# Attention and MoE on one core: the last chunk's stores cut into transfers of 32 rows on two queues, its two halves of tokens summed one after the other

## The chip, the cores and the metric

The kernel runs on one core of a Trainium2 chip. The metric is the device time of one execution in microseconds (us). The time before is 1025.86 us, the median of three runs (1025.6, 1025.86 and 1030.05).

## What is computed

The inputs are q, k and v, each 8 batches x 8 heads x 576 positions x 64, and the weights of a two-layer block. The attention is a sum of two parts, one over keys averaged in groups of four and one over a window of seven positions; its result, turned to 4608 tokens of 512 numbers, goes through the block:

```python
def _attn_ref(q, k, v):
    q_d = q.reshape(B, H, Sd, factor, D).mean(axis=3)        # k_d, v_d likewise
    out_up = np.repeat(sm_attn(q_d, k_d, v_d), factor, axis=2)
    mask = np.abs(pos[:, None] - pos[None, :]) < factor
    ...
    return (out_up + out_local).astype(np.float32)

def _moe_ref(x, w_in, w_out, alpha):                          # 4608x512, 512x2048, 2048x512
    h = x @ w_in
    g = np.maximum(h, 0.0) + alpha * np.minimum(h, 0.0)
    return (g @ w_out).astype(np.float32)
```

## The kernel before

The 4608 tokens are worked on in 18 chunks of 256 (`T`, `NCHUNK`). The hidden dimension of 2048 is taken in 8 pairs of 128 (`NP`), so that there are 144 steps (`NS`), eight to a chunk. One step has five parts: `hidden` (24 matmuls in three terms, since both factors are held as a high and a low part), `slopes` on ScalarE, `larger` on VectorE, `split` (the high part on ScalarE, the low part on GpSimd, the tiles `gh` and `gl`) and `product` (line 786), which multiplies by the second weight matrix and adds into two PSUM tiles of 128 tokens x 512, `o` in the profile. These two tiles are the two halves of tokens of a chunk, m = 0 and m = 1. They take the sum over all eight steps of the chunk.

The order of all instructions is written out by hand: each part is put down with a due time by `at`, in units of one step, and the list is sorted and emitted (lines 847 to 854 and 901 to 903). `finish` (line 799) stands 0.42 of a step after the last `product` of its chunk. Attention work for later chunks lies between the steps; it is all over before the last chunks, whose steps follow each other with nothing between.

In `product` (lines 791 to 797) the loops run over the two blocks j of the pair, the three terms i (`gh` with the high weights, `gh` with the low ones, `gl` with the high ones) and the two halves m, with m innermost. A step therefore issues 12 matmuls that go to the two PSUM tiles in turn, and the sums of both halves are complete only with the last two.

`finish` copies each half from PSUM to a staging tile `sg` on ScalarE (line 802) and stores it from SyncE's queue (line 805). Where the rows go is decided by `rows` (line 773). Tokens of the first 576 positions lie in the output's order, and their store is one run of rows. All later chunks hold their tokens in another order: 192 positions are six rows of the sequence by 32 places that are 18 rows apart. For these, `rows` yields patterns such as

```python
                u, o = divmod(pos, 192)
                m = min(n, 192 - o)
                row = (u // 3) * S + 6 * (u % 3) + o // 32
                ap = bass.AP(out.tensor, row * DM, [[DM, m // 32], [SEG * DM, 32], [1, DM]])
```

in which the outermost count is m // 32. The last chunk starts at position 4352, which is 128 positions into a group of 192. Its half m = 0 is stored as 64 rows (2 x 32) and then 64 rows of the next group (2 x 32), its half m = 1 as 128 rows (4 x 32). A row of the output is 2 KB, so these three transfers have 128, 128 and 256 KB. Chunks 0 and 1 are stored as runs of 128 rows.

Of the kernel before, what the change touches and what calls it, by code (L numbers as in the profile page):

```python
# [9 lines left out]
F32 = mybir.dt.float32  # L10
# [7 lines left out]
DM, DF = 512, 2048  # L18
# [7 lines left out]
NF = DF // 128  # L26
T = 256
# [6 lines left out]
SB = 2  # L34
# [16 lines left out]
def tile_attention_moe(ctx: ExitStack, tc: tile.TileContext, q, k, v, w_in, w_out, alpha, out):  # L51
    nc = tc.nc
# [3 lines left out]
    two = ctx.enter_context(tc.tile_pool(name="two", bufs=2))  # L56
# [17 lines left out]
    NS = NCHUNK * NF // 2  # L74
    NP = NF // 2
# [41 lines left out]
    wi, wo = ([[None] * 4, [None] * 4] for _ in range(2))  # L117
# [623 lines left out]
    gs, outs, hs = {}, {}, {}  # L741
# [31 lines left out]
    def rows(pos, n):  # L773
        while n:
            if pos < S:
                m = min(n, S - pos)
                ap = bass.AP(out.tensor, pos * DM, [[DM, m], [1, DM]])
            else:
# [4 lines that stand above are left out]
            yield m, ap  # L783
            pos, n = pos + m, n - m

    def product(st):
        c, fp = divmod(st, NP)
        if fp == 0:
            outs[c] = [ps_o.tile([128, DM], F32, tag="po", name=f"o{c}_{m}") for m in range(T // 128)]
        gh, gl = gs.pop(st)  # L790
        for j in range(2):
            f = 2 * fp + j
            n, o = divmod(f, 4)
            for i, (g, w) in enumerate(((gh, 0), (gh, 1), (gl, 0))):
                for m, po in enumerate(outs[c]):
                    nc.tensor.matmul(po, g[:, j, 128 * m:128 * m + 128], wo[w][n][:, o, :],  # L796
                                     start=(f == 0 and i == 0), stop=(f == NF - 1 and i == 2))

    def finish(c):
        for m, po in enumerate(outs.pop(c)):  # L800
            sg = two.tile([128, DM], F32, tag="stage", name=f"sg{c}_{m}", bufs=SB)
            nc.scalar.copy(sg, po)
            row = 0
            for cnt, ap in rows(T * c + 128 * m, 128):
                nc.sync.dma_start(ap, sg[row:row + cnt, :])
                row += cnt

    def place_rest():
        hi, lo = (t[:, :, 0:S - 2 * T] for t in operand(2))
        nc.scalar.copy(hi, rest)  # L810
        sub(lo, rest, f32(hi))
# [7 lines left out]
    with tc.tile_pool(name="start", bufs=1) as start:  # L819
        load_pair, load_windows, pair = first_batch(start)  # L820
        todo = [(w, fp) for fp in range(NP) for w in range(2)]
        for step in ORDER.split():
            kind, i = step[0], int(step[1])
# [16 lines left out]
        def at(t, f, *args):  # L840
            events.append((t, len(events), f, args))
# [5 lines left out]
    for s in range(NS):  # L847
        at(s - 1.95, hidden, s)
        at(s - 1.45, slopes, s)
        at(s - 1.15, larger, s)  # L850
        at(s - 1.0, split, s)
        at(s + 0.6, product, s)
        if s % NP == NP - 1:
            at(s + 1.02, finish, s // NP)

    blocks = [(w, fp, c) for w in range(2) for fp in range(N_EARLY, NP) for c in range(2)]
    at(-1.98, load_raw, 0, N_EARLY)
# [71 lines left out]
```

## Time and profile before

| what | value |
|---|---|
| median of three runs | 1025.86 us (1025.6 to 1030.05) |
| the profiled execution | 1026.39 us |
| its span, from the first to the last instruction | 1024.5 us |
| mean granted TensorE clock | 0.969 |
| TensorE busy | 960.5 us, 94% of the span |
| VectorE, ScalarE, GpSimd busy | 81%, 55%, 48% |
| share of the 16 DMA engines, last six of 40 slices of the span | 1 0 0 0 0 0 tenths |

The table's lines come from the page of the profile and its list of cores. The time of an execution is 1.89 us above its span, which lies around what the profiler sees. In the views, a row of the timeline gives the start in the span, the length, the engine, the line of the kernel, the operation, the tiles written and read and, behind an x, how many instructions it merges. A row of the table of windows gives a stretch of the span, its length, the busy time of each engine with its number of instructions, the granted clock, the share of the 16 DMA engines that were busy, and the GB/s that they moved; a share of 0.25 stands for four engines. `SPq` is SyncE's queue, on which line 805 issues; issuing instructions do not count as busy. Line 925 is the end of the program, where SyncE waits for the last transfers.

### The profile page before, as it was taken

The page shows a single profiled execution, that of the slowest core. Times are in us where ns is not written, and L with a number is a line of the kernel's source. Part 1 is how long each engine was busy: PE and PEld are TensorE (multiplying, and loading weights), DVE is VectorE, ACT ScalarE, POOL GpSimd, SP SyncE. Part 2 cuts the span into 40 slices and gives each one's busy share as a digit, 9 for nine tenths or more (in the row PEclk, how much of TensorE's full clock was granted, in tenths as well). Part 3 has the DMA queues.
Part 4 walks back from the last instruction along what each step waited for, and adds up shares of the span by engine and source line. Part 5 has one row for each costly group of instructions (what it writes and reads, how often), then busy time and mean ns, then how long its engine had stood idle before and what let it go on. Part 6 is the DMA issues. An engine that isn't in the chain of part 4 may idle for free.

```text
span 1024.5 us, 17852 instructions
## 1 busy us (share of the span) xinstructions
PE 960.5 (94%) x6402; PEld 853.0 (83%) x6402; DVE 831.8 (81%) x1346; ACT 560.4 (55%) x1484; POOL 487.7 (48%) x612
## 2 busy tenths in 40 slices
PE   4877989999999999999999999999999999999995
PEld 4756868898888899988888888888888898989894
DVE  6899978898788899899879888898898899995110
ACT  4767766465555554555555554655555564444442
POOL 2160645676565645555555544655555542333221
PEclk9956989999999999999999999999999999999998
DMA  8947343232322322322322232322322221100000
GB/s 184 228 141 246 111 126 110 96 109 85 115 100 95 106 75 86 109 93 102 107 84 74 92 107 77 116 90 80 104 98 81 93 78 62 73 36 21 1 21 20
DMA packets 59549, 98.25 MB, mean 96 GB/s; under 512 B 19910, under 2 KB 25286, under 8 KB 59462
## 3 DMA queue, kind: packets, MB, share of 16 engines
q1 hardware_dynamic: 59462, 97.12, 30.1%
q8 instruction: 50, 0.82, 0.3%
q14 instruction: 37, 0.30, 0.1%
HBM read 87.67 MB, written 9.44 MB: 95 GB/s over the span
## 4 chain that ended last, share of the span: by engine, by line
PE 74%; DVE 12%; DMA 4%; ACT 3%; issue 2%; SPq 2%; POOL 2%; ACTq 0%; DVEq 0%; POOLq 0%
PE h L752 34%; PE o L796 33%; PE s L263 2%; PE pv L297 2%; DVE temp L193 2%; DMA raw<-in_moe_w_in 1%; PE xp L659 1%; DMA ld<-in_v 1%; PE pT L287 1%; DVE temp L194 1%; DMA k<-in_k 1%; DVE t L764 1%; DVE qk L591 1%; SPq L393 1%; DVE temp L188 1%
## 5 line engine op out<-in xcount | busy, mean ns | idle before, releaser
L69 POOL TENSOR_TENSOR gl<-t,gh 128x512 fp32r<-128x512 f32 x144 | 186.4, 1295 | 312.9 <-ACT gh L769 281.5
L760 ACT ACTIVATE t<-h,slope 128x256 f32<-128x256 f32 x288 | 136.3, 473 | 205.4 <-PE h L752 163.6
L72 POOL TENSOR_TENSOR ld<-ld 72x256 f32<-72x256 f32 x168 | 130.8, 779 | 158.4 <-DMA ld<-in_q 88.6
L752 PE MATMUL h<-xh,wih 128*128 128x256 f32 x1152 | 191.9, 288 | 0.7 <-ACT xh L518 0.7
L764 DVE TENSOR_TENSOR t<-h,t 128x512 f32<-128x512 f32 x144 | 99.0, 687 | 114.8 <-ACT h L761 112.9
L796 PE MATMUL o<-woh,gh 128*128 128x512 f32 x576 | 187.5, 407 | 0.4 <-ACT woh L203 0.4
L752 PE MATMUL h<-xl,wih 128*128 128x256 f32 x1152 | 184.3, 282 | 1.4 <-POOL xl L69 1.4
L752 PE MATMUL h<-xh,wil 128*128 128x256 f32 x1152 | 185.0, 283 | 0.0
L796 PE MATMUL o<-woh,gl 128*128 128x512 f32 x576 | 181.1, 396 | 0.9 <-POOL gl L69 0.9
L796 PE MATMUL o<-wol,gh 128*128 128x512 f32 x576 | 181.4, 396 | 0.2 <-DVE wol L211 0.2
L752 PEld LDWEIGHTS h<-xh,wih 128*128 128x128 f32 x1152 | 164.2, 191 | 10.7 <-issue 1.8
L752 PEld LDWEIGHTS h<-xl,wih 128*128 128x128 f32 x1152 | 157.5, 190 | 1.6 <-POOL xl L69 1.6
L752 PEld LDWEIGHTS h<-xh,wil 128*128 128x128 f32 x1152 | 158.4, 191 | 0.0
L769 ACT CAST gh<-t 128x512 fp32r<-128x512 f32 x144 | 89.1, 619 | 120.7 <-DVE t L764 71.4
L595 DVE TENSOR_REDUCE ls<-qk 128x12 f32<-128x768 f32 (+1 forms) x126 | 136.4, 1082 | 2.8
L796 PEld LDWEIGHTS o<-woh,gl 128*128 128x128 f32 x576 | 108.2, 188 | 27.5 <-POOL gl L69 1.3
L796 PEld LDWEIGHTS o<-wol,gh 128*128 128x128 f32 x576 | 108.1, 188 | 26.8 <-DVE wol L211 1.1
L761 ACT ACTIVATE h<-h,sign 128x256 f32<-128x256 f32 x288 | 126.4, 439 | 0.0
L650 DVE TENSOR_TENSOR lb<-lb,pv 128x384 f32<-128x384 f32 x202 | 113.9, 564 | 5.5
L796 PEld LDWEIGHTS o<-woh,gh 128*128 128x128 f32 x576 | 98.1, 189 | 16.2 <-issue 2.2
L647 DVE TENSOR_TENSOR pv<-v,lb 128x1152 f32<-128x1152 f32 x84 | 93.6, 1115 | 2.6
L591 DVE TENSOR_TENSOR qk<-k,qp 128x768 f32<-128x768 f32 (+1 forms) x78 | 84.1, 1079 | 0.6 <-DMA k<-in_k 0.6
(146 smaller groups left out, 1108.6 us busy)
## 6 DMA issues: line engine op xcount, KB each, us to landing
k<-in_k SPq DMA_DIRECT2D x41, 384.0 KB
v<-in_v SPq DMA_DIRECT2D x41, 384.0 KB
raw<-in_moe_w_in SPq DMA_DIRECT2D x16, 512.0 KB
raw<-in_moe_w_out SPq DMA_DIRECT2D x16, 512.0 KB
ld<-in_q SPq DMA_DIRECT2D x56, 144.0 KB
ld<-in_k SPq DMA_DIRECT2D x56, 144.0 KB
ld<-in_v SPq DMA_DIRECT2D x56, 144.0 KB
q<-in_q SPq DMA_DIRECT2D x42, 192.0 KB
```

Source lines behind the costliest of these rows:

```text
L69: nc.gpsimd.tensor_tensor(o, a, b, op=ALU.subtract)
L72: nc.gpsimd.tensor_tensor(o, a, b, op=ALU.add)
L591: nc.vector.tensor_tensor(st["pr"][:, :nd], window(tiles[u, "k"], half, d0, nd), st["qp", half].unsqueeze(1).to_broadcast([128, nd, 2, 192 ...
L595: nc.vector.tensor_reduce(out=st["s"][:, half, d0:d0 + nd, :].rearrange("p a b -> p (a b)"), in_=st["pr"][:, :nd].rearrange("p a h (t d) - ...
L647: nc.vector.tensor_tensor(st["pr"][:, :nd], window4(tiles[u, "v"], half, d0, nd), prob(half, d0, nd), op=ALU.mult)
L650: nc.vector.tensor_tensor(st["acc"], st["acc"], st["pr"][:, i], op=ALU.add)
L752: nc.tensor.matmul(ph[:, j], w[:, m, 128 * o:128 * o + 128], x[:, m, :], start=(i == 0), stop=(i == 11))
L760: nc.scalar.activation(t[:, j], hs[st][:, j], AF.Copy, scale=slope[:, f:f + 1])
L761: nc.scalar.activation(hs[st][:, j], hs[st][:, j], AF.Copy, scale=sign[:, f:f + 1])
L764: nc.vector.tensor_tensor(gs[st], hs.pop(st), gs[st], op=ALU.max)
L769: nc.scalar.copy(gh, t)
L796: nc.tensor.matmul(po, g[:, j, 128 * m:128 * m + 128], wo[w][n][:, o, :], start=(f == 0 and i == 0), stop=(f == NF - 1 and i == 2))
```

## The change

Three things change, all in the last chunk alone. In the last step (`NS - 1`) `product` sorts its 12 matmuls by the half m, so that the six of m = 0 come first and the six of m = 1 after them; within a half, the order stays. In all other steps the order is the same as before. The last chunk is stored by a new function `finish_last`, at the same due time as `finish`: it copies half 0 on ScalarE and half 1 on VectorE, and it stores each half as four transfers of 32 rows (64 KB), the first and third from SyncE's queue and the second and fourth from ScalarE's queue. `rows` yields for 32 rows a pattern whose outermost count is 1: `[[DM, 1], [SEG * DM, 32], [1, DM]]`. No other transfer of the kernel is issued from ScalarE's queue.

```diff
-        for j in range(2):
+        order = [(j, i, m) for j in range(2) for i in range(3) for m in range(T // 128)]
+        if st == NS - 1:
+            order.sort(key=lambda x: x[2])
+        for j, i, m in order:
             f = 2 * fp + j
             n, o = divmod(f, 4)
-            for i, (g, w) in enumerate(((gh, 0), (gh, 1), (gl, 0))):
-                for m, po in enumerate(outs[c]):
-                    nc.tensor.matmul(po, g[:, j, 128 * m:128 * m + 128], wo[w][n][:, o, :],
-                                     start=(f == 0 and i == 0), stop=(f == NF - 1 and i == 2))
+            g, w = ((gh, 0), (gh, 1), (gl, 0))[i]
+            nc.tensor.matmul(outs[c][m], g[:, j, 128 * m:128 * m + 128], wo[w][n][:, o, :],
+                             start=(f == 0 and i == 0), stop=(f == NF - 1 and i == 2))
...
+    def finish_last(c):
+        for m, po in enumerate(outs.pop(c)):
+            sg = two.tile([128, DM], F32, tag="stage", name=f"sg{c}_{m}", bufs=SB)
+            if m == 0:
+                nc.scalar.copy(sg, po)
+            else:
+                nc.vector.tensor_copy(sg, po)
+            for i in range(4):
+                (_, ap), = rows(T * c + 128 * m + 32 * i, 32)
+                (nc.sync if i % 2 == 0 else nc.scalar).dma_start(ap, sg[32 * i:32 * i + 32, :])
...
-            at(s + 1.02, finish, s // NP)
+            at(s + 1.02, finish if s + 1 < NS else finish_last, s // NP)
```

## The prediction

> **What bounds the kernel now.** The edit touches only the last step of the last chunk and its stores, so the profile is read there. I started with the page's head, then took the timeline of the last microseconds.
>
> ```profile
> span 1024.5 us, 17852 instructions
> ```
> ```profile
> 1009.45 0.63 PE L796 MATMUL o<-woh,gh 128*128 128x512 f32 x2
> 1011.78 0.62 PE L796 MATMUL o<-woh,gl 128*128 128x512 f32 x2
> 1012.22 1.07 ACT L802 COPY sg<-o 128x512 f32<-128x512 f32 x2 [4.95 <-PE o L796]
> 1012.83 1.79 SPq L805 DMA_DIRECT2D out<-sg  x3
> ```
>
> Of the last product's twelve matmuls the first pair and the last pair are shown: the 11th starts 2.33 us after the first, so 0.233 us lie from one to the next. TensorE is done at 1012.4. The two copies end at 1013.29, the three stores are issued by 1014.62, and yet the span goes on to 1024.5. So 11.2 us from the last copy on have no engine at work. The chain of waits that ended last stops at ScalarE's queue and shows nothing of this; the waits of SyncE and the instructions of the program's end do.
>
> ```profile
> SPq L925 <- DMA out<-sg: 8.8, 3, 3.5
> ```
> ```profile
> L925 SPq EVENT_SEMAPHORE  x1: 28/28/28, 1018.2 to 1018.2; - x1
> L925 SPq EVENT_SEMAPHORE  x1: 28/28/28, 1021.1 to 1021.1; - x1
> L925 SPq EVENT_SEMAPHORE  x1: 28/28/28, 1023.6 to 1023.6; - x1
> ```
>
> The three releases (last two fields: when) are the landings of the three stores, at 1018.2, 1021.1 and 1023.6. The landing at 1023.6 ends the kernel, and 0.9 us of closing work follow. What sets these landings is seen in windows cut at the right places: first the stores of chunk 0, then those of chunk 16, then the tail.
>
> ```profile
> 162.20:163.00 0.80, 0.00 (x0) 0.00 (x0) 0.80 (x2) 0.80 (x3) 0.80 (x1) 1.00 0.00 0
> 163.00:164.40 1.40, 1.33 (x9) 1.18 (x10) 1.37 (x2) 1.37 (x5) 0.02 (x1) 1.00 1.01 350
> 975.00:977.00 2.00, 2.00 (x15) 1.77 (x14) 0.00 (x0) 0.91 (x3) 0.00 (x0) 1.00 0.21 22
> 977.00:982.00 5.00, 5.00 (x35) 4.60 (x34) 0.69 (x1) 1.64 (x4) 1.29 (x1) 1.00 0.25 93
> 1013.00:1014.00 1.00, 0.00 (x0) 0.00 (x0) 0.00 (x0) 0.29 (x1) 0.00 (x0) 1.00 0.00 0
> 1014.00:1016.00 2.00, 0.00 (x0) 0.00 (x0) 0.00 (x0) 0.00 (x0) 0.00 (x0) 0.65 0.12 25
> 1016.00:1021.50 5.50, 0.00 (x0) 0.00 (x0) 0.00 (x0) 0.00 (x0) 0.00 (x0) 0.50 0.23 71
> 1021.50:1023.00 1.50, 0.00 (x0) 0.00 (x0) 0.00 (x0) 0.00 (x0) 0.00 (x0) 0.50 0.13 51
> 1023.00:1023.20 0.20, 0.00 (x0) 0.00 (x0) 0.00 (x0) 0.00 (x0) 0.00 (x0) 0.50 0.13 51
> 1023.20:1024.50 1.30, 0.00 (x0) 0.00 (x0) 0.00 (x0) 0.00 (x0) 0.00 (x0) 0.50 0.00 0
> ```
>
> The last two fields are the share of the 16 DMA engines and the GB/s. Chunk 0's stores, runs of 128 rows, fill all 16 engines (1.01, 350 GB/s). Chunk 16's, whose outermost count is 4, run on four (0.25, 93 GB/s). The tail has two stores of outermost count 2 and one of 4: it runs at up to four engines (0.23) and ends on two (0.13, 51 GB/s). So the outermost count of the pattern is the number of engines, and they are the same ones each time: two engines carry 32 + 32 + 32 = 96 of the last chunk's 256 rows each. 96 rows of 2 KB at 25.5 GB/s (half of 51) are 7.7 us, and the 9.2 us from 1014.0 to 1023.2 are these plus a slow start, which is the row of 1014 to 1016 (25 GB/s). Bound now: two DMA engines, after all compute is over.
>
> **The change part by part.** Further rows for the prices:
>
> ```profile
> 1007.35 1.29 POOL L69 TENSOR_TENSOR gl<-t,gh 128x512 fp32r<-128x512 f32 x1 [4.30 <-ACT gh L769]
> ```
> ```profile
> 1012.22 0.59 ACT L802 COPY sg<-o 128x512 f32<-128x512 f32 x1 [4.95 <-PE o L796]
> ```
> ```profile
> 1009.45 0.40 PE L796 MATMUL o<-woh,gh 128*128 128x512 f32 x1
> ```
> ```profile
> 1012.83 0.55 SPq L805 DMA_DIRECT2D out<-sg  x1
> ```
> ```profile
> L764 DVE TENSOR_TENSOR t<-h,t 128x512 f32<-128x512 f32 x144 | 99.0, 687 | 114.8 <-ACT h L761 112.9 <-POOL pv L627 0.8 <-POOL xl L69 0.3
> L653 DVE TENSOR_TENSOR x<-lb,pv 128x384 f32<-128x384 f32 x42 | 23.4, 557 | 6.0 <-POOL pv L72 2.2
> ```
> ```profile
> 162.18 0.85 SPq L805 DMA_DIRECT2D out<-sg  x2
> ```
> ```profile
> 944.00:974.00 30.00, 30.00 (x194) 27.09 (x193) 4.15 (x6) 12.23 (x28) 6.77 (x6) 1.00 0.00 1
> 983.00:1012.00 29.00, 29.00 (x173) 25.53 (x173) 3.45 (x5) 9.94 (x23) 6.47 (x5) 1.00 0.00 1
> ```
> ```profile
> 897.04 0.78 SPq L545 DMA_DIRECT2D v<-in_v  x1
> 899.81 0.23 SPq L547 DMA_DIRECT2D v<-in_v  x1
> ```
> ```profile
> 1001.21 2.80 PE h L752 x24
> ```
>
> *The order of the sums.* Twelve matmuls stay twelve, so half 1 is complete at 1012.41 as now. Half 0 is complete with the sixth matmul: it starts at 1009.45 + 5 x 0.233 = 1010.62 and ends 0.40 later at 1011.02, where now the 11th ends at 1011.78 + 0.40 = 1012.18. That is 1.16 us earlier. Two things could spoil it. The third matmul now needs `gl` (at 1009.92, where it was the fifth, at 1010.38); GpSimd has it at 1007.35 + 1.29 = 1008.64, so 1.28 us of cover are left. And six matmuls in a row add into one PSUM tile instead of two in turn. `hidden` does that already, twelve in a row into one region, and its 24 matmuls of half the width take 2.80 us, the same 0.117 us per 256 columns as 0.233 per 512. I take nothing for it.
>
> *The copies.* Now ScalarE starts 0.04 us after half 0 is summed (1012.22 against 1012.18), copies for 0.59 and the issue follows 0.02 to 0.03 later. After the change: copy 1011.06 to 1011.65, stores of half 0 issued from 1011.68. Half 1 goes to VectorE, which has nothing left to do. A copy of 128x512 from PSUM by VectorE is not in the trace; the nearest rows are 0.56 (three quarters of the width, two operands) and 0.69 (`larger`, the same width, from PSUM). I take 0.69: 1012.45 to 1013.14, issue at 1013.17. ScalarE's second copy ended at 1013.29, so this gains 0.15.
>
> *The issues.* Eight in place of three, four on each queue. On SyncE one takes 0.23 to 0.78 us by the rows; a three-level pattern like these takes 0.55, and 0.57 from start to start. ScalarE issues none in this trace; I price its issues as SyncE's, 0.57, with the same bounds. Half 0's are then at 1011.68 and 1012.25 on each queue, over by 1012.82, ahead of half 1's, at 1013.17 and 1013.74. On ScalarE the second pair waits for VectorE's copy, but behind it stands only the end of the program. The same holds on SyncE. From an issue to the first bytes the tail shows 1.17 us (1012.83 to 1014.0), chunk 0 shows 0.8. So the first bytes move at 1012.85, and the last transfer's can start at 1013.74 + 1.17 = 1014.91.
>
> *The data.* 32 rows have an outermost count of 1, then 32 with a step. Taken as 32, they can be dealt to 16 engines, two rows each, and all eight transfers put 16 rows on every engine instead of 96 on two. This is the term that matters, and the trace shows 16 engines for stores only in a pattern without the leading 1. At chunk 0's rate 524 KB take 524 / 350 = 1.50 us. Whether the slow start comes back is open: chunk 0's stores, after a short pause, have none; chunks 16 and 17, each after some 30 us with next to no transfer (1 GB/s in the rows from 944 and from 983), both have it, 2.0 us at 22 and 25 GB/s, whether four engines take part or two. I take it as it stands there, 2.0 us in which 50 KB move, so from 1012.85 to 1014.85. Then 474 KB at 350 GB/s take 1.35 us: last bytes at 1016.2. This is later than the 1014.91 + 0.37 (two transfers, 131 KB at 350) = 1015.28 which the issues allow, so a wrong price of an issue or of VectorE's copy is hidden up to 0.9 us.
>
> [...]
>
> *The end.* From the last bytes (1023.2) to SyncE's release (1023.6) are 0.4 us, and 0.9 to the end of the span. So: 1016.2 + 0.4 + 0.9 = 1017.5 in place of 1024.5, **7.0 us less**. The profiled execution took 1026.39, and its forecast is 1019.4. It stands 0.53 above the median of 1025.86; the forecast of the median is **1018.9 us**. Without the slow start the issues bind: 1015.28 + 1.3 = 1016.6, 7.9 less, 1018.0; with issues at 0.23 another 0.3 less, and with chunk 0's 0.8 to the first bytes 0.4 less, 1017.3.
>
> **The rivals.** A measurement of this kernel can tell about 0.5%, 5.1 us, from no change; faster is below 1020.7, slower above 1031.
>
> *One queue's worth of issues.* If the two queues share what makes their transfers, or ScalarE issues at half speed, the eight issues follow each other: half 0's until 1011.68 + 4 x 0.57 = 1013.96, half 1's last at 1013.96 + 3 x 0.57 = 1015.67, first bytes at 1016.84, 64 KB in 0.19, then 1.3: 1018.3. That is 6.2 us less, 1019.7, still faster. For it: nothing here shows two queues at once. [...] Chance 0.15.
>
> *A slow start for each half.* If the slow start belongs to each new burst or to each queue's first use, half 0 takes 1012.85 + 2.0 + (262 - 50) / 350 = 1015.46, and half 1 the same 2.61 again, 1018.07, with the end 1019.4: 5.1 less, 1020.8, right at the bound. Against it: in the tail of before the third store, issued at 1014.1, shows no second slow stretch (71 GB/s from 1016 on). For it: twelve engines and a queue that have been idle for long. Chance 0.12, half of it faster and half the same.
>
> *One engine.* The counts 2, 4 and 128 gave 2, 4 and 16 engines; a count of 1 may give one. Then 256 rows go over one engine: 50 KB in the slow start to 1014.85, 474 KB at 25.5 GB/s 18.6 us, 1033.4, with the end 1034.7: 10.2 more, 1036.1. It decides at two engines: with two, 474 / 51 = 9.3 us end at 1025.4, about as now. For it: the rule as the trace shows it, taken to the letter. Against it: a count of one deals out nothing, and 32 stands next to it. Chance 0.06, slower.
>
> *The cut is worth nothing.* If smaller transfers still wait on the same engines for the same 9.2 us, only the earlier start counts: 1.16 us less, 1024.7, the same. [...] Chance 0.03.
>
> **How the numbers follow.** The forecast has 0.64. Faster: 0.64 + 0.15 + 0.06 = 0.85; the same 0.06 + 0.03 = 0.09; slower 0.06. The range goes from 1017.2, a little below the case without slow start and with cheap issues, to 1021.0, which takes in both rivals above the forecast; one engine and the last rival, 0.09, stay outside, and the rest to 0.2 is for the scatter of runs (one of before is at 1030.05).
>
> **What would show it.** Right: half 0's copy starts near 1011.06, VectorE's takes about 0.69, four issues stand on ScalarE's queue at about 0.55, the DMA share goes to 0.9 or more after a slow first stretch, and SyncE's last release comes near 1016.6. Wrong: a share of 0.06 for 20 us (one engine), issues on ScalarE of over 1.1 us or in turn with SyncE's, a second slow stretch near 1015, or a last release after 1018.5, which would leave less than 5.1 us.

## The result, and the profile after

The changed kernel took 1022.28 us, the median of 16 runs (1017.95 to 1030.71). The kernel before, run beside it, took 1029.08 us, also the median of 16 (1025.6 to 1035.75). The ratio is 0.9934, with a 95% interval from 0.9912 to 0.9956: faster by 0.66%, or 6.8 us (4.5 to 9.1 by the interval). The forecast was a gain of 7.0 us and a time of 1018.9 us, with a range from 1017.2 to 1021.0. So the gain came about as forecast, and the time lies 1.3 us above the range, because the time that the gain was taken from was not 1025.86. One later run of the changed kernel, 1181.21 us at a granted clock of 0.749, is left out of its median and ratio below.

The profiled execution of the changed kernel took 1021.87 us with a span of 1020.0. That span is 4.5 us shorter, not 7. To see why, the span is cut in two at the end of the last matmul. First the timeline of the end of the changed kernel (columns as before; SPq and ACTq are the two queues that issue transfers):

```profile
span 1020.0 us, 17859 instructions
```
```profile
1013.71 0.59 ACT L815 COPY sg<-o 128x512 f32<-128x512 f32 x1 [3.78 <-PE o L798]
1014.32 2.29 SPq L820 DMA_DIRECT2D out<-sg  x4
1014.32 2.36 ACTq L820 DMA_DIRECT2D out<-sg  x4
...
1014.67 0.40 PE L798 MATMUL o<-woh,gl 128*128 128x512 f32 x1
1015.11 0.69 DVE L817 COPY sg<-o 128x512 f32<-128x512 f32 x1 [5.89 <-PE o L798]
```

The last matmul ends at 1015.07, and the span goes on for 1020.0 - 1015.07 = 4.9 us. Before, it ended at 1011.78 + 0.62 = 1012.40 and the span went on for 12.1 us. This stretch, called the tail from here on, became 7.2 us shorter. But the last matmul itself came 2.7 us later. Nothing that the change touches lies ahead of it except the order of its own step. Where the 2.7 us arose is seen by the copies that close chunks 10, 11 and 16 (counted from 0), before (line 802) and after (line 804, the same line of the kernel after the edit):

```profile
680.31 1.07 ACT L802 COPY sg<-o 128x512 f32<-128x512 f32 x2
...
733.18 1.06 ACT L802 COPY sg<-o 128x512 f32<-128x512 f32 x2
...
973.51 1.06 ACT L802 COPY sg<-o 128x512 f32<-128x512 f32 x2
```
```profile
681.39 1.07 ACT L804 COPY sg<-o 128x512 f32<-128x512 f32 x2
...
735.84 1.06 ACT L804 COPY sg<-o 128x512 f32<-128x512 f32 x2
...
976.17 1.06 ACT L804 COPY sg<-o 128x512 f32<-128x512 f32 x2
```

The changed kernel is 1.08 us late at 681, 2.66 at 736, and 2.66 still at 976. The windows between the first two, before and then after, show what goes with the second step: TensorE's granted clock (third field from the end) fell for some 8 us in the second execution (0.83 and 0.74) and not in the first (1.00), which costs about 0.17 x 4 + 0.26 x 4 = 1.7 us by an estimate from these clocks alone; the step between the two copies is 1.58 us.

```profile
684.00:688.00 4.00, 2.60 (x15) 2.16 (x15) 3.60 (x10) 2.66 (x9) 0.00 (x0) 1.00 0.33 99
688.00:692.00 4.00, 4.00 (x33) 3.87 (x32) 3.29 (x5) 0.96 (x2) 2.97 (x4) 1.00 0.38 136
```
```profile
684.00:688.00 4.00, 2.60 (x18) 1.95 (x18) 3.53 (x13) 3.44 (x11) 0.49 (x1) 0.83 0.35 104
688.00:692.00 4.00, 4.00 (x18) 3.29 (x17) 3.83 (x6) 0.69 (x2) 0.35 (x1) 0.74 0.42 138
```

Such a fall is not peculiar to the changed kernel: near 535 us both profiles show one (0.79 and 0.78 in the two windows of 4 us from 531 on before, 0.76 and 0.82 after), each worth about 1.7 us by the same estimate. Whether the one near 688 would have come without the change, these two profiles don't show. The first 1.08 us arose ahead of 631 us without such a difference of the clock: the changed kernel was still 0.53 us early at the stores of chunk 8 (issued from 578.61, before from 579.14) and 1.08 late at those of chunk 9 (631.87 against 630.79), and from 544 to 632 the clock was 1.00 in both profiles. This was not traced. In the profiles of all kernels told of here the last matmul ends anywhere from 1010.6 to 1016.3 us. The tails of the two kernels that were profiled twice came back within 0.1 us. All experiments are therefore read by their tails. But two kernels with the same code in the tail can differ by 1.0 us there, as the last experiment shows, so a difference of less than that is not put down to an edit with certainty. The windows of the changed tail:

```profile
1014.30:1015.10 0.80, 0.77 (x4) 0.29 (x2) 0.00 (x0) 0.00 (x0) 0.00 (x0) 1.00 0.00 0
1015.10:1016.30 1.20, 0.00 (x0) 0.00 (x0) 0.69 (x1) 0.00 (x0) 0.00 (x0) 1.00 0.86 219
1016.30:1016.60 0.30, 0.00 (x0) 0.00 (x0) 0.00 (x0) 0.00 (x0) 0.00 (x0) 1.00 0.01 0
1016.60:1017.80 1.20, 0.00 (x0) 0.00 (x0) 0.00 (x0) 0.00 (x0) 0.00 (x0) 0.98 0.86 220
1017.80:1018.40 0.60, 0.00 (x0) 0.00 (x0) 0.00 (x0) 0.00 (x0) 0.00 (x0) 0.50 0.07 10
1018.40:1020.00 1.60, 0.00 (x0) 0.00 (x0) 0.00 (x0) 0.00 (x0) 0.00 (x0) 0.50 0.00 0
```

The share stands at 0.86 where it was 0.12 to 0.23. The view of DMA queues for the tail, before and then after, says the same in another way: before there were 256 rows and 8 short packets, as many as the three transfers had engines (2 + 2 + 4). Now the short packets are 128, which is 16 for each of eight transfers. The one packet more belongs to an instruction transfer, of which more below.

```profile
DMA packets 264, 0.52 MB, mean 46 GB/s; under 512 B 8, under 2 KB 8, under 8 KB 264
```
```profile
DMA packets 385, 0.53 MB, mean 107 GB/s; under 512 B 128, under 2 KB 128, under 8 KB 384
```

### The profile page after: what moved, and what is told of

It is laid out like the page before. It is cut to its first block, busy times and chain, and to the rows that moved or that the text cites. A ratio compares the mean times of both kernels' runs of the same rounds, so it can differ in the third digit from the quotient of the medians.

```text
span 1020.0 us, 17859 instructions
## 1 busy us (share of the span) xinstructions
PE 961.8 (94%) x6402; PEld 853.0 (84%) x6402; DVE 832.9 (82%) x1347; ACT 560.0 (55%) x1483; POOL 487.6 (48%) x612
## 4 chain that ended last, share of the span: by engine, by line
PE 71%; DVE 12%; DMA 5%; ACT 5%; issue 2%; POOL 2%; SPq 2%; ACTq 0%; DVEq 0%; POOLq 0%
PE h L752 33%; PE o L798 32%; DMA ld<-in_v 3%; PE s L263 2%; PE pv L297 1%; DVE temp L193 1%; DVE t L764 1%; PE xp L659 1%; DVE qk L591 1%; DMA k<-in_k 1%; PE pT L287 1%; DVE temp L194 1%; DVE ls L595 1%; ACT t L760 1%; DMA raw<-in_moe_w_in 1%
## 5 line engine op out<-in xcount | busy, mean ns | idle before, releaser
L72 POOL TENSOR_TENSOR ld<-ld 72x256 f32<-72x256 f32 x168 | 130.7, 778 | 154.7 <-DMA ld<-in_q 78.7
```

The lines of the kernel that those rows point to most:

```text
L72: nc.gpsimd.tensor_tensor(o, a, b, op=ALU.add)
```

## The experiments

The theory was that the number of DMA engines that carry the last rows is nearly the whole gain. Its rivals were the earlier sum of half 0 with the second queue, and, for the slow start, engines that had been idle. Each tail below is the end of the span less the end of the last matmul (start plus length of the last matmul row).

**The cut alone.** The changed kernel with the new order, VectorE's copy and the second queue undone.

```diff
-        if st == NS - 1:
-            order.sort(key=lambda x: x[2])
...
-            if m == 0:
-                nc.scalar.copy(sg, po)
-            else:
-                nc.vector.tensor_copy(sg, po)
+            nc.scalar.copy(sg, po)
...
-                (nc.sync if i % 2 == 0 else nc.scalar).dma_start(ap, sg[32 * i:32 * i + 32, :])
+                nc.sync.dma_start(ap, sg[32 * i:32 * i + 32, :])
```

> The last chunk's stores in transfers of 32 rows, all eight from SyncE; the order of the sums and both copies on ScalarE as before. Read as the tail, from the end of the last matmul to the end of the span: 12.1 us before, 4.9 us after the change. Theory (the number of DMA engines that carry the rows is nearly the whole gain): eight issues one behind the other at 0.39 us from 0.43 on, the last starts 3.2 us after the last matmul, then 2.75 to the release and 1.0 to the end as in the changed kernel: tail 6.9 us, time 5 us below before. Rival (the gain is the earlier sum and the second queue): the cut alone leaves the tail at 11 us or more and the time unchanged.

```profile
span 1022.4 us, 17857 instructions
```
```profile
1015.37 0.62 PE L796 MATMUL o<-woh,gl 128*128 128x512 f32 x2
...
1016.41 3.62 SPq L815 DMA_DIRECT2D out<-sg  x8
```
```profile
1017.20:1020.90 3.70, 0.00 (x0) 0.00 (x0) 0.00 (x0) 0.00 (x0) 0.00 (x0) 0.72 0.57 142
```

The tail is 1022.4 - 1015.99 = 6.4 us, 5.7 of the 7.2 us. The time was 1023.01 us against 1027.34, ratio 0.9961 (0.9941 to 0.9982). Eight issues in 3.62 us set the pace: 64 KB every 0.45 us are 145 GB/s, near the 142 of the window. On top of the cut, the order, VectorE's copy and the second queue together bring the remaining 1.5 us.

**All but the cut.** The changed kernel with the transfers of before, dealt to the two queues in turn.

```diff
-            for i in range(4):
-                (_, ap), = rows(T * c + 128 * m + 32 * i, 32)
-                (nc.sync if i % 2 == 0 else nc.scalar).dma_start(ap, sg[32 * i:32 * i + 32, :])
+            row = 0
+            for i, (cnt, ap) in enumerate(rows(T * c + 128 * m, 128)):
+                (nc.sync if i % 2 == 0 else nc.scalar).dma_start(ap, sg[row:row + cnt, :])
+                row += cnt
```

> The changed kernel with the transfers of before (64, 64 and 128 rows): sums one after the other, half 1 copied by VectorE, stores dealt to two queues in turn. Theory: two engines still carry 96 rows each, so only the earlier start of half 0 counts, 1.2 us: tail 10.9 us, time about 1 us below before. Rival (the gain is the earlier sum and the second queue): tail 5 to 6 us, time 6 us below before.

```profile
span 1023.7 us, 17854 instructions
```
```profile
1011.42 0.40 PE L798 MATMUL o<-woh,gl 128*128 128x512 f32 x1
```
```profile
1012.70:1014.70 2.00, 0.00 (x0) 0.00 (x0) 0.00 (x0) 0.00 (x0) 0.00 (x0) 0.89 0.12 35
1014.70:1016.70 2.00, 0.00 (x0) 0.00 (x0) 0.00 (x0) 0.00 (x0) 0.00 (x0) 0.50 0.22 29
1016.70:1020.20 3.50, 0.00 (x0) 0.00 (x0) 0.00 (x0) 0.00 (x0) 0.00 (x0) 0.50 0.25 84
```

The tail is 11.9 us, and the time did not move: 1027.47 us, ratio 1.0007 (0.9981 to 1.0034). The theory expected 10.9. Half 0 did start earlier, but a second slow stretch (29 GB/s) came with half 1; that it took the 1.2 us back fits, and was not tested by itself. The rival that gave the gain to order and queue falls.

**The old order.** The changed kernel without the sort of the last step.

```diff
-        if st == NS - 1:
-            order.sort(key=lambda x: x[2])
```

> The changed kernel with the old order of the last step's matmuls (the halves in turn). Theory: the last two issues of each queue wait behind half 0's, which come 1.2 us later; the last one starts 1.7 instead of 1.2 us after the last matmul: tail 5.4 us against 4.9. Rival (the order is worth the 1.2 us by which half 0 is earlier): 6.1 us.

```profile
span 1018.7 us, 17859 instructions
```
```profile
1012.62 0.63 PE L796 MATMUL o<-woh,gl 128*128 128x512 f32 x2
```

The tail is 1018.7 - 1013.25 = 5.45 us, 0.5 longer than the changed kernel's, near the theory's 5.4 and not the rival's 6.1. The size is uncertain: the last issue on ScalarE took 0.89 us here, where the others took 0.40 to 0.44, and that alone is about as long as the difference.

**One queue.** The changed kernel with all transfers from SyncE.

```diff
-                (nc.sync if i % 2 == 0 else nc.scalar).dma_start(ap, sg[32 * i:32 * i + 32, :])
+                nc.sync.dma_start(ap, sg[32 * i:32 * i + 32, :])
```

> The changed kernel with all eight transfers issued by SyncE. Theory: half 0's four issues end 0.8 us after the last matmul, half 1's last one starts at 2.0 instead of 1.2 us: tail 5.7 us against 4.9. Rival (both queues feed the same engines, so the second is worth nothing): 4.9 us.

```profile
span 1021.4 us, 17858 instructions
```
```profile
1015.35 3.60 SPq L820 DMA_DIRECT2D out<-sg  x8
...
1015.71 0.40 PE L798 MATMUL o<-woh,gl 128*128 128x512 f32 x1
```

The tail is 5.3 us, 0.4 longer than the changed kernel's, half of what the theory said. So small a difference, from one profile, doesn't rule out the rival.

**Runs of 128 rows.** The kernel before, with each half of the last chunk stored as one run of 128 rows; these rows land in other places of the output than they should.

```diff
-            for cnt, ap in rows(T * c + 128 * m, 128):
+            p0 = T * c + 128 * m
+            run = [(128, bass.AP(out.tensor, p0 * DM, [[DM, 128], [1, DM]]))]
+            for cnt, ap in (run if c == NCHUNK - 1 else rows(p0, 128)):
```

> The kernel before, but each half of the last chunk stored as one run of 128 rows (outermost count 128, as chunks 0 and 1 are), so these rows land in other places of the output than they should. Sums, copies and queue as before; two issues instead of three. Theory (number of engines): issues at 0.4 and 0.9 us after the last matmul, first bytes at 1.2, 524 KB at 350 GB/s to 2.8, 0.6 to the release and 1.0 to the end: tail 4.5 us without any cut, second queue or new order. Rival (small transfers are what helps): tail of 8 us or more; with a slow start as before 5.5 to 6.5.

```profile
span 1020.5 us, 17852 instructions
```
```profile
1015.72 0.62 PE L796 MATMUL o<-woh,gl 128*128 128x512 f32 x2
...
1016.76 0.85 SPq L807 DMA_DIRECT2D out<-sg  x2
```
```profile
1017.60:1019.00 1.40, 0.00 (x0) 0.00 (x0) 0.00 (x0) 0.00 (x0) 0.00 (x0) 0.93 0.98 369
```

The tail is 4.2 us with the old order, one queue, ScalarE's copies and only two issues. Against the cut alone (6.4 us), which has the same order, queue and copies, that is 2.2 us less. So here two transfers of 256 KB were no hindrance (share 0.98, 369 GB/s), and eight of 64 KB from the same queue were no help in themselves (0.57, 142 GB/s); the cut is one way to a pattern that uses 16 engines.

**Runs of 122 and 6 rows.** The same with each half as two runs, the larger of 122 = 2 x 61 rows. These rows too land in other places than they should.

```diff
+            run = [(n, bass.AP(out.tensor, (p0 + r) * DM, [[DM, n], [1, DM]])) for r, n in ((0, 122), (122, 6))]
```

> The kernel before, each half of the last chunk stored as two runs of neighbouring rows, 122 and 6, so these rows land in other places of the output than they should. By the counts 122 rows go to two engines (122 = 2 x 61). Theory (the number of engines sets the tail, whatever the pattern): 124 rows of 2 KB on each of two engines at 25.5 GB/s take 9.9 us, tail 12.8 us, with a slow start 13.8; against 4.2 measured for one run of 128. The slow start: if it belongs to few engines, the first 2 us move about 50 KB again; if it belongs to patterns of three levels (2 or 4 groups of rows 18 apart), they move the full 100 KB. Rival (contiguous rows are what made the runs of 128 quick): tail about 4.5 us.

```profile
span 1029.7 us, 17854 instructions
```
```profile
1014.86 0.62 PE L796 MATMUL o<-woh,gl 128*128 128x512 f32 x2
```
```profile
1016.80:1018.80 2.00, 0.00 (x0) 0.00 (x0) 0.00 (x0) 0.00 (x0) 0.00 (x0) 0.92 0.22 32
1018.80:1027.50 8.70, 0.00 (x0) 0.00 (x0) 0.00 (x0) 0.00 (x0) 0.00 (x0) 0.50 0.14 49
```

The tail is 1029.7 - 1015.48 = 14.2 us. Neighbouring rows from the same queue, but a share of 0.14, two engines, and 49 GB/s, where the runs of 128 rows had 0.98 and 369. The short packets in this tail are 16, as many as two for each run of 122 rows and six for each run of 6 make. That 122 rows go to two engines was the author's estimate until this run; it shows that neither a large count of rows nor their being neighbours was enough for 16. The slow start is there too (32 GB/s for 2 us), so in this run it came without a pattern of three levels.

**Engines kept awake.** The kernel before, with a load of 768 KB that nobody reads just ahead of the last stores.

```diff
+    def awake():
+        kt = late.tile([128, 2, 12, 64], F32, tag="kt", name="awake")
+        flat = kt.rearrange("p h t d -> p (h t d)")
+        nc.gpsimd.memset(flat[:, 0:1], 0.0)
+        nc.sync.dma_start(flat, bass.AP(q.tensor, 0, [[1536, 128], [1, 1536]]))
+
+    at(NS - 1 - 0.9, awake)
```

> The kernel before with one load of 768 KB on 16 engines put ahead of the last chunk's stores, released by GpSimd after the last low part, so that the DMA engines are busy until about 1 us before the first store. Its data is read by nobody. Theory a (the slow start comes from engines that were idle for long): the first 2 us of the stores move about 100 KB instead of 50, and the tail goes from 12.1 to about 11.1 us. Theory b (it belongs to transfers dealt to two or four engines, as the changed kernel's quick start after the same idle time suggests): slow start and tail stay, 12.1 us.

```profile
1007.60:1010.80 3.20, 3.02 (x13) 2.09 (x12) 0.00 (x0) 0.37 (x1) 0.00 (x0) 1.00 0.68 246
1010.80:1012.00 1.20, 0.00 (x0) 0.00 (x0) 0.00 (x0) 0.70 (x2) 0.00 (x0) 1.00 0.00 0
1012.00:1014.00 2.00, 0.00 (x0) 0.00 (x0) 0.00 (x0) 0.00 (x0) 0.00 (x0) 0.84 0.11 20
```

The engines worked until 1010.8, and the stores still began at 20 GB/s. The tail was 11.7 us (span 1022.3, last matmul over at 1010.61), 0.4 less than before. So idleness of over 1.2 us isn't needed for the slow start.

**Both copies on ScalarE.** The changed kernel without VectorE's copy.

```diff
-            if m == 0:
-                nc.scalar.copy(sg, po)
-            else:
-                nc.vector.tensor_copy(sg, po)
+            nc.scalar.copy(sg, po)
```

> The changed kernel with both halves copied by ScalarE (half 1 no longer by VectorE); order, transfers and queues as changed. ScalarE's copy takes 0.59 against VectorE's 0.69 us and comes free 0.1 us before it is needed, so by the copies alone the tail would be 4.8 against 4.9 us. Besides this: in both profiles of the changed kernel an instruction transfer runs among the last rows, and the last two rows of its DMA engine come 0.3 us apart, 0.6 us behind all others; the kernel with the loads cut as well has no such transfer there and a tail of 3.9. Theory (VectorE's additional instruction draws that transfer): it is gone and the tail is 3.8 to 4.0 us. Rival (VectorE's copy has nothing to do with it): the transfer stays and the tail is 4.7 to 4.9.

```profile
span 1020.0 us, 17858 instructions
```
```profile
1015.27 0.40 PE L798 MATMUL o<-woh,gl 128*128 128x512 f32 x1
...
1015.88 0.58 ACT L814 COPY sg<-o 128x512 f32<-128x512 f32 x1 [0.99 <-PE o L798]
```

The tail is 4.3 us against 4.9, although the copy starts 0.2 us late behind ScalarE's own issues. The instruction transfer is gone from among the rows, and so is the gap ahead of the last of them. The time was 1020.51 us, ratio 0.9917 (0.9887 to 0.9947), which cannot be told from the changed kernel's. The tail did not fall to the 3.8 to 4.0 that was expected. Nor does VectorE's copy by itself draw the transfer in: the kernel with the loads cut (below) has the copy, no transfer there, and a tail of 3.9 to 4.0 us, 0.3 to 0.4 less than this one. So the longer tail of the changed kernel goes with the transfer, and not with the copy. That the transfer causes it is not shown, and what draws it in is open.

**Tokens by place.** The changed kernel with the last chunk's tokens reordered when `gh` and `gl` are made, so that 64 rows have an outermost count of 32.

```diff
+        if st >= NS - NP:
+            t = t.rearrange("p j (g a b) -> p (j g) b a", a=2, b=32)
+            gh, gl = (x.rearrange("p j (g b a) -> p (j g) b a", a=2, b=32) for x in (gh, gl))
...
+            for i in range(2):
+                (_, ap), = rows(T * c + 128 * m + 64 * i, 64)
+                ap = bass.AP(out.tensor, ap.offset, [[SEG * DM, 32], [1, 2 * DM]])
+                (nc.sync if i == 0 else nc.scalar).dma_start(ap.rearrange("b (a d) -> b a d", a=2), sg[64 * i:64 * i + 64, :])
```

> The changed kernel with the tokens of the last chunk put in another order when the high and low parts are made (two neighbouring rows side by side), so that a transfer of 64 rows has an outermost count of 32: one issue per queue and half in place of two. Theory (engines, and behind them the issues on the path): the last issue starts 0.8 instead of 1.2 us after the last matmul, tail 4.2 to 4.5 us against 4.9. Rival (transfers of 64 rows are slower in themselves): tail of 4.9 us or more. In the time of the whole kernel the two differ too little to tell.

The tail was 4.8 us (span 1017.0, last matmul over at 1012.20), no better: an issue of this pattern took 0.55 to 0.65 us, which eats most of what the saved one was worth. An instruction transfer and late last rows are in this tail too, so the two cannot be weighed against each other. Ratio 0.9913 (0.9882 to 0.9944).

**The loads cut as well.** The changed kernel with the loads of q, k and v for the later batches in transfers of 32 partitions. The edit for k and v is shown, that for q is alike.

```diff
-                nc.sync.dma_start(flat, bass.AP(src.tensor, off,
-                                                [[2 * HEAD, 4], [SEG * D, 32], [1, 768]]))
+                for a in range(4):
+                    nc.sync.dma_start(flat[32 * a:32 * a + 32],
+                                      bass.AP(src.tensor, off + a * 2 * HEAD, [[SEG * D, 32], [1, 768]]))
```

> The changed kernel with the loads of q, k and v for all later batches cut the same way, into transfers of 32 partitions, all from SyncE. Theory (four engines are too few for these loads as well, and GpSimd's waits for loads behind them reach TensorE): these waits shrink and the last matmul ends 2 to 5 us earlier, ratio to before 0.989 to 0.992. Rival (these loads lie off the path, and four times as many issues clog SyncE's queue): last matmul not earlier, ratio 0.993 or above.

It took 1019.75 us, ratio 0.9905 (0.9875 to 0.9935). GpSimd's waits for loads of q went from 78.7 us in the changed kernel (88.6 before) to 56.4, but the last matmul ended at 1013.58, in the middle of the others. The tail was 3.9 us. To tell it from the changed kernel both ran once more side by side:

> The changed kernel once more, beside the one with the loads in transfers of 32 partitions as well. If the tail is what the change is worth, about 7 us of 1029: ratio 0.993, tail between 3.9 and 4.9 us.

> The changed kernel with the loads of q, k and v in transfers of 32 partitions, once more. If more engines for these loads help the body: ratio 0.003 or more below that of the changed kernel in the same call. If the loads lie off the path: within 0.002 of it.

The changed kernel took 1020.93 us (seven runs), ratio 0.9923 (0.9895 to 0.9951), tail 4.9; the one with the loads cut 1018.83, ratio 0.9903 (0.9874 to 0.9933), tail 4.0. The ratios are 0.002 apart, just at the bound that was set, and half of that is the tail, in whose code the two don't differ. A gain in the body is not shown.

**The tails together.** The instruction transfer is a row `q14 instruction` in the view of DMA queues. This table says where one fell among the last rows.

| kernel | tail, us | instruction transfer among the last rows |
|---|---|---|
| before | 12.1 | no |
| all but the cut | 11.9 | yes |
| the cut alone | 6.4 | no |
| changed (two profiles) | 4.9, 4.9 | yes |
| old order | 5.45 | yes |
| one queue | 5.3 | yes |
| tokens by place | 4.8 | yes |
| both copies on ScalarE | 4.3 | no |
| runs of 128 rows | 4.2 | no |
| the loads cut as well (two profiles) | 3.9, 4.0 | no |
| engines kept awake | 11.7 | no |
| runs of 122 and 6 rows | 14.2 | no |

The changed kernel and the one with the loads cut have the same code for the tail, and 1.0 us lies between them. The steps of 2 us and more in the table are well above this. The worths of the order and of the second queue, each read by itself, are not. Taken together they are: between the cut alone and both copies on ScalarE, which have no such transfer and differ in the order and the second queue, lie 2.1 us.

## Why the prediction was right and its range wrong

*What bounds the end.* Right. Two engines carried 96 rows each (0.13 and 51 GB/s at the end of before), and giving the rows to 16 engines (0.86 and 220 GB/s) took 7.2 us off the tail, forecast 7.0. The cut alone gives 5.7 of it and all else without the cut 0.2. One sum there was loose: 7.7 us and a slow start, which costs about 1.0 us (50 KB in 2.0 us instead of at 51 GB/s), make 8.7 and not 9.2.

*The pattern with a leading 1.* It was dealt to 16 engines; the rival of one engine falls by the share of 0.86 and the 128 short packets. That 32 rows go to 16 engines was the author's estimate; no store of the kernel before has that count, and the changed kernel shows it. In the stores looked at here, outermost counts of 2 (share 0.13), 4 (0.25) and 122 (0.14) went with two or four engines, counts of 32 (0.86) and 128 (1.01 for chunk 0, 0.98 for the last chunk) with 16. So the outermost count is not by itself the number of engines; what sets this number for other counts was not shown.

*Order, copies, issues.* Half 0's copy began 1.36 us before the end of the last matmul, forecast 1.35; VectorE's took 0.69 us, forecast 0.69. ScalarE's issues took 0.38 to 0.44 us and SyncE's 0.31 to 0.41, forecast 0.55; that price came from patterns of three levels, with a leading 2 or 4, and the other pattern of three levels, that of the tokens by place, took 0.55 to 0.65 again.

*The data and the end.* Here several terms were off, and that 7.0 came so near to 7.2 is luck: they cancelled. The slow start of 2.0 us did not come: the first 1.2 us moved 219 GB/s. The first bytes came 0.8 us after the issue, not 1.17. Against this the rate was 220 GB/s, not 350, with a pause of 0.3 us between the halves, and the last few rows came 0.6 us behind the others. Counted from the end of the last matmul, the last bytes came at 3.2 us instead of 3.8, the last release at 3.9 instead of 4.2, and the end of the span at 4.9 instead of 5.1. Without the slow start the prediction's own sum ends at 4.2, or 3.8 with the quicker first bytes; the kernel with the loads cut, whose tail has the same code and no instruction transfer, ends at 3.9 to 4.0. So about 1 us that the sum took for a slow start was made up by late rows and a later release that nobody forecast. The term that set the end in the sum, 50 KB in the slow start, was a mistake in kind: it was read as a property of an idle DMA, and the runs show it with two or four engines (20 to 35 GB/s over 2.0 us), whether these had just worked or not, and show none with 16 (191 GB/s in the first 0.3 us of the changed kernel's tail, 336 in the first 0.5 us of chunk 0's stores). Why few engines started slowly is open.

*The rivals.* The two queues did not issue in turn: both had four issues between 1014.32 and 1016.7, each of 0.31 to 0.44 us. With all on one queue the tail was 0.4 us longer, forecast 0.8. The slow start for each half exists, in the kernel without the cut, not in the changed one. The cut was not worth nothing: alone it took 5.7 us off the tail, where the transfers before did not use all engines (0.12 to 0.23). Where one run of 128 rows does use them (0.98), the tail with no cut is 2.2 us shorter than that of the cut alone (4.2 against 6.4).

*How the numbers follow.* This is the step that failed: the base of the sum, "the median of 1025.86", from which 7.0 us were taken. It was a median of three runs, though one of the three was 1030.05. Over 16 runs the median is 1029.08, 3.2 us more, and in the later comparisons 1027.34 to 1030.42. Runs of one kernel spread over some 10 us; the profiles show the end of the last matmul anywhere within 5.7 us, so at least that much of it lies in the body. The prediction had seen the scatter and gave it a chance of 0.11 outside its range, but no width within it: the bound at 1021.0 was set by the rivals. From 1029.08 the same sum gives 1022.1; 1022.28 was measured.

*What would show it.* One sign that was set for being wrong did come: a last release after 1018.5. The release in the profile stands at 1019.0:

```profile
L939 SPq EVENT_SEMAPHORE  x1: 28/28/28, 1019.0 to 1019.0; - x1
```

The bound was set on the clock of one execution, whose last matmul ended at 1012.4. In this one it ended at 1015.07, and the release came 3.9 us behind it, where 4.2 had been forecast. The sign had the same fault as the range.

## What to carry to other kernels

Nothing hid the last stores of this kernel (a tail of 12.1 us before), so look at such a place at the share of DMA engines and the GB/s: a share of two or four sixteenths went here with outermost counts of 2 (0.13), 4 (0.25) and 122 (0.14), and counts of 32 (0.86) and 128 (0.98) used all 16. That was worth more than the reordering ahead of it (5.7 us of the tail against 0.2 for all else without the cut). Cut only as far as the pattern needs, since issues of 0.3 to 0.6 us can stand in the path one behind the other (eight took 3.62 us on one queue). And when one number of a few runs is the base of a forecast, give the range the spread of these runs, or forecast the difference alone.

## What was not expected of the hardware

- Transfers dealt to two or four engines began with 2 us at 20 to 35 GB/s, also 1.2 us after other transfers (20 GB/s with the engines kept awake) and a second time within one tail (35 and then 29 GB/s with all but the cut).
- Transfers of 64 KB from two queues together moved 220 GB/s, two runs of 128 rows from one queue 369 GB/s.
- With runs of 122 rows queued on two engines, an issue of 6 rows on SyncE took 3.08 us; the shortest of the four took 0.24, and their median is 0.31. Long issues are not peculiar to that: in the kernel before, one store of an earlier chunk took 3.65 us to issue.

```profile
L807 SPq DMA_DIRECT2D out<-sg x4: 237/314/3075, 1015.9 to 1017.0; - x4
```

- An instruction transfer among the last rows went with two rows that came 0.6 us behind the others, and with a tail 1.0 us longer than the same code had without it. The row of it in the changed kernel, in the window from 1017.4 to 1017.5:

```profile
q14 instruction: 1, 0.01, 19.3%
```
